# Linear attention with RMS norm, then a gated feed-forward block: token-major attention, one GELU per tile, per-batch token blocks, a written order

## The chip, the core and the metric

One core of one Trainium2 chip runs the whole kernel. The metric is the time of one execution on the device, in microseconds (us). Five engines run their own instruction streams and meet at semaphores: TensorE (PE; its weight loads are listed as PEld), VectorE (DVE), ScalarE (ACT), GpSimd (POOL) and SyncE (SP). TensorE writes its results to PSUM, from which ACT and DVE read them.

## What is computed

```python
def _attn_ref(q, k, v, g_norm):          # 8 batches, 8 heads, 576 tokens, head size 64
    kv = np.einsum('bhsd,bhse->bhde', k, v)
    out = np.einsum('bhsd,bhde->bhse', q, kv)
    rms = np.sqrt(np.mean(out * out, axis=-1, keepdims=True) + 1e-06)
    return (out / rms * g_norm)
# x = the heads of a token side by side: 4608 tokens x 512
def _moe_ref(x, w_gate, w_val, w_out, w_res):   # 512x1536, 512x1536, 1536x512, 512x512
    g = x @ w_gate
    gelu = 0.5 * g * (1.0 + erf(g / sqrt(2)))
    ffn_out = gelu * (x @ w_val) @ w_out
    res_gate = 1.0 / (1.0 + np.exp(-(x @ w_res)))
    return x + res_gate * ffn_out
```

All inputs and the output are float32 in memory; the loads convert to fp16, in which the matrix products run.

## The kernel before

**Attention** (`attention_batch`, L189 to L248) works channel-major. Per batch, POOL issues fifteen loads: q in five token chunks of 128, 128, 128, 128 and 64 rows (L195), then k (L200) and v (L204) alternating over the same chunks. q has two buffers, k and v have one each. For each of four pairs of heads, TensorE sums k^T v over the five chunks (L212), DVE masks the two cross-head blocks and multiplies by g_norm (L220), TensorE transposes q (L223) and ACT copies the transpose out (L225). For each half of the 576 tokens follow the product with q (L229, channels on the partitions), a copy (L231) and a square (L234) on DVE, a matmul that sums the squares over the channels of a head and spreads the sum back (L236), and a copy (L237). At the end of the batch ACT takes Ln and Exp of all these sums (L238, L240), with a table load for each, and DVE multiplies and so writes `xT` (L243): 512 channels by all 4608 tokens, kept for the whole run.

**Feed-forward.** Tokens go in nine blocks of 512, which do not fall on batch borders. `moe_gval` (L111 to L151) takes twelve slices of 128 of the 1536 hidden units. A slice has four matmuls for the gate (L121), four for the value (L130), a copy of the gate on ACT (L138), gate times value on DVE (L140), the square of the gate on POOL (L142), two DVE steps (L144, L148), a Sigmoid on ACT (L150) and a last product on DVE (L151): the GELU is built from a cubic and a Sigmoid. The gate and value tiles share three PSUM buffers. `moe_out` (L152 to L186) takes the four 128-token pieces of a block: twelve matmuls with w_out (L159), four with w_res (L168), four transposes that bring x back to token-major (L177), a Sigmoid (L179), a copy (L181), a product on DVE (L183), the residual add on POOL (L185) and the store on SP's queue (L186). The first two share two PSUM buffers.

**Order.** `attention_batch` 0 and 1, the four weight loads (L105 to L108, whole matrices) and `moe_gval(0)` come first; then each round has the attention of batch b+2, `moe_gval(b+1)` and `moe_out(b)`. This is the order in the program text; the framework's scheduler reorders instructions on every engine by priority and by what it takes to be ready.

Of the kernel before, what the change touches and what calls it, by code (L numbers as in the profile page):

```python
# [19 lines left out]
def kernel(  # L21
# [11 lines left out]
):  # L33
    nc = tc.nc
    P = nc.NUM_PARTITIONS
    B, H, S, D = q.shape
    T = B * S
# [23 lines left out]
    qt2p = ctx.enter_context(tc.tile_pool(name="qt2p", bufs=4))
    moep = ctx.enter_context(tc.tile_pool(name="moep", bufs=2))
    finp = ctx.enter_context(tc.tile_pool(name="finp", bufs=2))

    pmoe = ctx.enter_context(tc.tile_pool(name="pmoe", bufs=3, space=bass.MemoryType.PSUM))
    pattn = ctx.enter_context(tc.tile_pool(name="pattn", bufs=1, space=bass.MemoryType.PSUM))

    ident32 = consts.tile([P, P], FP32, tag="ident32")
    make_identity(nc, ident32)
    ident = consts.tile([P, P], FP16, tag="ident")  # L70
    nc.vector.tensor_copy(out=ident, in_=ident32)

    gcol = consts.tile([P, 1], FP32, tag="gcol")
    nc.sync.dma_start(out=gcol[0:D, :], in_=g_norm.unsqueeze(1))
    nc.sync.dma_start(out=gcol[D : 2 * D, :], in_=g_norm.unsqueeze(1))
    ginv2 = consts.tile([P, 1], FP32, tag="ginv2")
    nc.vector.tensor_tensor(out=ginv2, in0=gcol, in1=gcol, op=ALU.mult)
    nc.vector.reciprocal(out=ginv2, in_=ginv2)

    jmask = consts.tile([P, P], FP32, tag="jmask")  # L80
    nc.gpsimd.memset(jmask, 0.0)
    nc.vector.memset(jmask[0:D, 0:D], 1.0)
# [7 lines left out]
    JG = consts.tile([P, P], FP16, tag="JG")  # L90
    nc.vector.tensor_tensor(out=JG, in0=jmask, in1=grow.rearrange("p a d -> p (a d)"), op=ALU.mult)
    JIG2 = consts.tile([P, P], FP16, tag="JIG2")
    nc.vector.tensor_scalar(
        out=JIG2, in0=jmask, scalar1=ginv2[:, 0:1], scalar2=None, op0=ALU.mult
    )
    eps_col = consts.tile([P, 1], FP32, tag="eps_col")
    nc.vector.memset(eps_col, RMS_EPS)

    wg16 = wpool.tile([P, 4, F], FP16, tag="wg16")
    wv16 = wpool.tile([P, 4, F], FP16, tag="wv16")  # L100
# [12 lines left out]

    def moe_gval(J: int):
        t0 = 512 * J
        hid = hidp.tile([P, NF, 512], FP16, tag="hid")
        hids[J] = hid
        for Fi in range(NF):
            gps = pmoe.tile([P, 512], FP32, tag="gval")
            for cc in range(4):  # L120
                nc.tensor.matmul(  # L121
                    gps,
                    lhsT=wg16[:, cc, Fi * P : (Fi + 1) * P],
                    rhs=xT[:, cc, t0 : t0 + 512],
                    start=(cc == 0),
                    stop=(cc == 3),
                )
            vps = pmoe.tile([P, 512], FP32, tag="gval")
            for cc in range(4):
                nc.tensor.matmul(  # L130
                    vps,
                    lhsT=wv16[:, cc, Fi * P : (Fi + 1) * P],
                    rhs=xT[:, cc, t0 : t0 + 512],
                    start=(cc == 0),
                    stop=(cc == 3),
                )
            g16 = moep.tile([P, 512], FP16, tag="g16")
            nc.scalar.copy(out=g16, in_=gps)  # L138
            gv = moep.tile([P, 512], FP16, tag="gv")
            nc.vector.tensor_tensor(out=gv, in0=g16, in1=vps, op=ALU.mult)  # L140
            x2 = moep.tile([P, 512], FP16, tag="x2")
            nc.gpsimd.tensor_tensor(out=x2, in0=g16, in1=g16, op=ALU.mult)  # L142
            w3 = moep.tile([P, 512], FP16, tag="w3")
            nc.vector.tensor_scalar(  # L144
                out=w3, in0=x2, scalar1=B_CUBE, scalar2=1.0, op0=ALU.mult, op1=ALU.add
            )
            z3 = moep.tile([P, 512], FP16, tag="z3")
            nc.vector.tensor_tensor(out=z3, in0=w3, in1=g16, op=ALU.mult)  # L148
            sg = moep.tile([P, 512], FP16, tag="sg")
            nc.scalar.activation(out=sg, in_=z3, func=AF.Sigmoid, scale=A_SIG)  # L150
            nc.vector.tensor_tensor(out=hid[:, Fi, :], in0=gv, in1=sg, op=ALU.mult)  # L151
    def moe_out(J: int):  # L152
        t0 = 512 * J
        hid = hids[J]
        for tci in range(4):
            tt0 = t0 + 128 * tci
            fps = pmoe.tile([P, 512], FP32, tag="fr", bufs=2)
            for Fi in range(NF):
                nc.tensor.matmul(  # L159
                    fps,  # L160
                    lhsT=hid[:, Fi, tci * 128 : (tci + 1) * 128],
                    rhs=wo16[:, Fi, :],
                    start=(Fi == 0),
                    stop=(Fi == NF - 1),
                )
            rps = pmoe.tile([P, 512], FP32, tag="fr", bufs=2)
            for cc in range(4):
                nc.tensor.matmul(  # L168
                    rps,
                    lhsT=xT[:, cc, tt0 : tt0 + 128],  # L170
                    rhs=wr16[:, cc, :],
                    start=(cc == 0),
                    stop=(cc == 3),
                )
            xps = pattn.tile([P, 4, 128], FP16, tag="ort", bufs=2)
            for cc in range(4):
                nc.tensor.transpose(xps[:, cc, :], xT[:, cc, tt0 : tt0 + 128], ident)  # L177
            sig = finp.tile([P, 512], FP32, tag="sig")
            nc.scalar.activation(out=sig, in_=rps, func=AF.Sigmoid)  # L179
            xsb = finp.tile([P, 512], FP16, tag="xsb")  # L180
            nc.scalar.copy(out=xsb, in_=xps)  # L181
            pf = finp.tile([P, 512], FP32, tag="pf")
            nc.vector.tensor_tensor(out=pf, in0=fps, in1=sig, op=ALU.mult)  # L183
            osb = finp.tile([P, 512], FP32, tag="osb")
            nc.gpsimd.tensor_tensor(out=osb, in0=pf, in1=xsb, op=ALU.add)  # L185
            nc.sync.dma_start(out=out[tt0 : tt0 + 128, :], in_=osb)  # L186
# [103 lines left out]
```

## Time and profile before

| what | value |
|---|---|
| median of 3 runs | 538.26 us (538.15 to 538.30) |
| span of the profiled execution, first to last instruction | 536.4 us |
| mean granted TensorE clock, share of full | 0.954 |
| matmuls, of 512 columns / of fewer | 1440 / 592 |
| busy share PE, DVE, ACT, POOL | 76%, 66%, 48%, 49% |

The profile gives a span; the execution as timed is longer by what lies around the span. A busy PE is not PE at its peak, because matmuls overlap: what a matmul costs in a dense stretch is read from the distance between the starts of groups.

### The profile page before, as it was taken

How to read it: one execution, taken by the hardware profiler on the slowest of the kernel's cores; microseconds unless marked ns; L12 is line 12 of the kernel's file. 1: busy time of each engine (PE TensorE's matmuls, PEld its weight loads, DVE VectorE, ACT ScalarE, POOL GpSimd, SP SyncE). 2: the span in 40 equal slices, each digit the busy share in tenths (PEclk: the TensorE clock that was granted, in tenths of full speed). 3: DMA queues.
4: the chain of work that ended last, by engine and by line, in shares of the span. 5: the costliest groups of instructions: out<-in, count | busy, mean ns of one | idle time of the engine just before them, and what ended most of it. 6: DMA issues, size and time to landing. Idle time of an engine off the chain costs nothing.

```text
span 536.4 us, 6023 instructions
## 1 busy us (share of the span) xinstructions
PE 405.8 (76%) x2032; PEld 189.5 (35%) x2032; DVE 355.6 (66%) x764; ACT 256.4 (48%) x368; POOL 263.6 (49%) x275
## 2 busy tenths in 40 slices
PE   0355877884998598869886889589859977987884
PEld 0121433431443244324433444235323433433442
DVE  0162887996878766956695859584958498389311
ACT  0024466458536743494248533853485344334321
POOL 8643783493469335934484448153314443343222
PEclk9999997997999898979989998999988999999999
DMA  9999990094049205930395019101000100100111
GB/s 84 149 201 172 120 107 7 5 102 47 20 61 99 34 20 66 82 24 21 69 88 36 21 59 83 7 20 40 20 1 20 59 2 0 57 23 2 39 59 60
DMA packets 121295, 29.30 MB, mean 55 GB/s; under 512 B 113584, under 2 KB 115632, under 8 KB 121264
## 3 DMA queue, kind: packets, MB, share of 16 engines
q0 software_dynamic: 115648, 19.41, 47.4%
q1 hardware_dynamic: 5616, 9.51, 4.8%
q8 instruction: 16, 0.26, 0.2%
q14 instruction: 15, 0.12, 0.1%
HBM read 38.86 MB, written 9.44 MB: 90 GB/s over the span
## 4 chain that ended last, share of the span: by engine, by line
DVE 35%; PE 26%; issue 13%; ACT 11%; POOL 7%; DMA 7%; POOLq 0%; ACTq 0%; DVEq 0%
PE fps L159 9%; DVE z L148 8%; DVE hid L151 7%; DVE w L144 6%; PE gps L121 6%; PE vps L130 4%; DVE gv L140 4%; ACT sg L150 4%; DMA wv<-in_moe_w_val_dram 3%; DVE sq L234 3%; POOL x L142 3%; DVE rbs L237 3%; PE rps L168 3%; ACT L150 3%; DVE og L231 2%
## 5 line engine op out<-in xcount | busy, mean ns | idle before, releaser
L142 POOL TENSOR_TENSOR x<-g 128x512 f16<-128x512 f16 x108 | 116.5, 1083 | 163.7 <-ACT g L138 155.9
L130 PE MATMUL vps<-xT,wv 128*128 128x512 f16 x432 | 126.6, 407 | 32.0 <-ACT g L138 31.7
L121 PE MATMUL gps<-xT,wg 128*128 128x512 f16 x432 | 124.3, 405 | 19.4 <-DVE gv L140 19.0
L150 ACT ACTIVATE sg<-z 128x512 f16<-128x512 f16 x108 | 68.0, 630 | 121.8 <-DVE z L148 121.6
L159 PE MATMUL fps<-wo,hid 128*128 128x512 f16 x432 | 103.8, 379 | 9.6 <-ACT sig L179 6.5
L185 POOL TENSOR_TENSOR osb<-pf,xsb 128x512 f32<-128x512 f32 x36 | 42.0, 1167 | 86.7 <-DVE pf L183 60.9
L138 ACT CAST g<-gps 128x512 f16<-128x512 f32 x108 | 61.5, 578 | 31.5 <-PE gps L121 28.1
L140 DVE TENSOR_TENSOR gv<-g,vps 128x512 f16<-128x512 f16 x108 | 73.2, 678 | 4.6 <-PE vps L130 3.6
L130 PEld LDWEIGHTS <-wv 128*128 128x128 f16 x432 | 42.9, 102 | 83.6 <-issue 45.7
L121 PEld LDWEIGHTS <-wg 128*128 128x128 f16 x432 | 42.7, 103 | 83.9 <-issue 48.4
L151 DVE TENSOR_TENSOR hid<-gv,sg 128x512 f16<-128x512 f16 x108 | 61.3, 568 | 16.5 <-ACT sg L150 14.6
L148 DVE TENSOR_TENSOR z<-w,g 128x512 f16<-128x512 f16 x108 | 61.7, 571 | 2.5
L159 PEld LDWEIGHTS <-hid 128*128 128x128 f16 x432 | 41.7, 98 | 59.5 <-issue 10.1
L144 DVE TENSOR_SCALAR w<-x 128x512 f16<-128x512 f16 x108 | 50.2, 466 | 8.9 <-POOL x L142 8.9
L183 DVE TENSOR_TENSOR pf<-fps,sig 128x512 f32<-128x512 f32 x36 | 24.7, 687 | 41.7 <-ACT sig L179 41.6
L212 PE MATMUL kvps<-v_sb,k_sb 128*128 128x128 f16 (+1 forms) x160 | 21.5, 231 | 30.8 <-DMA v_sb<-in_v_dram 29.3
L237 DVE COPY rbs<-rb 128x288 f32<-128x288 f32 x64 | 28.9, 451 | 20.1 <-PE rb L236 19.8
L179 ACT ACTIVATE sig<-rps 128x512 f32<-128x512 f32 x36 | 21.5, 597 | 42.3 <-PE rps L168 42.2
L200 POOL DMA_DIRECT2D k_sb<-in_k_dram x40 | 35.0, 875 | 12.8 <-PE kvps L212 10.8
L225 ACT COPY qt<-qtps 128x576 f16<-128x576 f16 x32 | 20.3, 634 | 43.7 <-PE qtps L223 43.6
L231 DVE CAST og<-otg 128x288 f16<-128x288 f32 x64 | 28.6, 447 | 18.4 <-PE otg L229 18.4
L236 PE MATMUL rb<-sq,JIG 128*128 128x288 f16 x64 | 19.7, 308 | 26.8 <-DVE sq L234 26.8
(41 smaller groups left out, 384.2 us busy)
## 6 DMA issues: line engine op xcount, KB each, us to landing
out_dram<-osb SPq DMA_DIRECT2D x36, 256.0 KB, 2.0
q_sb<-in_q_dram POOLq DMA_DIRECT2D x32, 128.0 KB, 4.4
k_sb<-in_k_dram POOLq DMA_DIRECT2D x32, 128.0 KB, 4.3
v_sb<-in_v_dram POOLq DMA_DIRECT2D x32, 128.0 KB, 4.4
wg<-in_moe_w_gate_dram POOLq DMA_DIRECT2D x1, 1536.0 KB, 12.1
wv<-in_moe_w_val_dram POOLq DMA_DIRECT2D x1, 1536.0 KB, 18.6
wo<-in_moe_w_out_dram POOLq DMA_DIRECT2D x1, 1536.0 KB, 12.8
q_sb<-in_q_dram POOLq DMA_DIRECT2D x8, 64.0 KB, 4.2
```

What stands on the lines that cost most here:

```text
L121: nc.tensor.matmul(gps, lhsT=wg16[:, cc, Fi * P : (Fi + 1) * P], rhs=xT[:, cc, t0 : t0 + 512], start=(cc == 0), stop=(cc == 3),)
L130: nc.tensor.matmul(vps, lhsT=wv16[:, cc, Fi * P : (Fi + 1) * P], rhs=xT[:, cc, t0 : t0 + 512], start=(cc == 0), stop=(cc == 3),)
L138: nc.scalar.copy(out=g16, in_=gps)
L140: nc.vector.tensor_tensor(out=gv, in0=g16, in1=vps, op=ALU.mult)
L142: nc.gpsimd.tensor_tensor(out=x2, in0=g16, in1=g16, op=ALU.mult)
L144: nc.vector.tensor_scalar(out=w3, in0=x2, scalar1=B_CUBE, scalar2=1.0, op0=ALU.mult, op1=ALU.add)
L148: nc.vector.tensor_tensor(out=z3, in0=w3, in1=g16, op=ALU.mult)
L150: nc.scalar.activation(out=sg, in_=z3, func=AF.Sigmoid, scale=A_SIG)
L151: nc.vector.tensor_tensor(out=hid[:, Fi, :], in0=gv, in1=sg, op=ALU.mult)
L159: nc.tensor.matmul(fps, lhsT=hid[:, Fi, tci * 128 : (tci + 1) * 128], rhs=wo16[:, Fi, :], start=(Fi == 0), stop=(Fi == NF - 1),)
L185: nc.gpsimd.tensor_tensor(out=osb, in0=pf, in1=xsb, op=ALU.add)
L237: nc.vector.tensor_copy(out=rbs[:, j, hh, :], in_=rb)
```

## The change

The kernel is rewritten, with the same loads from memory to fp16 and the same feed-forward products.

- Tokens are regrouped: block b (0 to 7) holds the first 512 tokens of batch b, and block 8 the last 64 tokens of each of the eight batches. k and v rests are padded with zeros to 128 rows; the rests of two batches' q share one 128-row tile.
- Attention is token-major: q is transposed, and the product (`a_o`) has tokens on the partitions. ACT copies it out and squares it, DVE reduces the square per head, and a 13-instruction DVE chain on 32 or 40 columns (`a_norm`) finds the inverse root by an integer shift and three Newton steps. Two DVE products give x (`a_x`), four transposes and an ACT copy give `xT` (`a_xT`). The matmul that summed squares, Ln and Exp are gone.
- The GELU is one ACT instruction out of PSUM and one DVE product. The gate's Sigmoid is a Tanh; two DVE instructions finish the output, and no transpose back is needed. POOL computes nothing except a set-up step: it issues loads.
- PSUM: six buffers for all feed-forward products in rotation, two for attention.
- The order is as written, on every engine (`manual_schedule`): sixteen slots per block, with a step of the next batch's attention behind the products of each slot. The loads of batch 0 come first, then the weights (gate and value in six column pieces each), then batch 1; batch b+2 is loaded from the start of block b.

Cut to its core (what was removed is shown above):

```diff
+    ctx.enter_context(tc.manual_schedule())
+    nc.scalar.preload_act_table_set("gelu_and_others")
...
+    load_batch(0)
...
+    load_weights()
+    load_batch(1)
...
+    def a_qT(b, jj):
+        ps = pattn.tile([P, 2, NP, P], FP16, tag="at", name="qtp")
+        for e in range(2):
+            j = 2 * jj + e
+            for pr in range(NP):
+                nc.tensor.transpose(ps[:, e, pr, :], q_sb[:, j, pr * P : (pr + 1) * P], ident)
+        nc.scalar.copy(out=st[b]["qT"][:, 2 * jj : 2 * jj + 2, :, :], in_=ps)
...
+    def a_kv(b):
+        ps = pattn.tile([P, NP, P], FP32, tag="at", name="kvp")
+        for pr in range(NP):
+            cs = slice(pr * P, (pr + 1) * P)
+            for j in range(NJ):
+                nc.tensor.matmul(ps[:, pr, :], lhsT=k_sb[:, j, cs], rhs=v_sb[:, j, cs], start=(j == 0), stop=False)
+            nc.tensor.matmul(ps[:, pr, :], lhsT=kr_z[b % 2][:, cs], rhs=vr_z[b % 2][:, cs], start=False, stop=True)
+        nc.vector.tensor_tensor(out=st[b]["kv2"], in0=ps, in1=mask[:, None, :].to_broadcast([P, NP, P]), op=ALU.mult)
...
+    def a_post_o(b, j, ps):
+        nc.scalar.copy(out=o32, in_=ps)
+        nc.scalar.activation(out=sq, in_=ps, func=AF.Square)
+        nc.vector.tensor_reduce(out=s["ss"][:, j, :], in_=sq, op=ALU.add, axis=mybir.AxisListType.X)
...
+    def a_norm(b):
+        nc.vector.tensor_scalar(out=m, in0=ss, scalar1=1.0 / D, scalar2=RMS_EPS, op0=ALU.mult, op1=ALU.add)
...
+        for _ in range(3):
+            nc.vector.tensor_tensor(out=a, in0=yy, in1=yy, op=ALU.mult)
+            nc.vector.tensor_tensor(out=a, in0=a, in1=mh, op=ALU.mult)
+            nc.vector.scalar_tensor_tensor(out=yy, in0=a, scalar=1.5, in1=yy, op0=ALU.add, op1=ALU.mult)
...
+            0: [lambda: attn_begin(b), lambda: a_qT(b, 0)],
+            1: [lambda: a_qT(b, 1)],
+            2: [lambda: a_kv(b)],
+            3: [lambda: a_rem_qT(b)] if odd else [],
+            4: [lambda: a_o(b, 0)],
+            5: [lambda: a_o(b, 1)],
+            6: [lambda: a_o(b, 2)],
+            7: [lambda: a_o(b, 3)],
+            8: [lambda: a_rem_o(b)] if odd else [],
+            9: [lambda: a_norm(b), lambda: a_x(b, 0)],
+            10: [lambda: a_x(b, 1)],
+            11: [lambda: a_x(b, 2), lambda: a_xT(b, 0)],
+            12: [lambda: a_x(b, 3), lambda: a_xT(b, 1)],
+            13: [lambda: a_xT(b, 2)] + ([lambda: a_x(b, 4)] if odd else []),
+            14: [lambda: a_xT(b, 3)],
+            15: [lambda: a_xT(b, 4)] if odd else [],
...
+    def m_gval(blk, f):
...
+        nc.scalar.activation(out=ge, in_=gps, func=AF.Gelu)
+        nc.vector.tensor_tensor(out=hids[blk][:, f, :], in0=ge, in1=vps, op=ALU.mult)
...
+        nc.scalar.activation(out=th, in_=rps, func=AF.Tanh, scale=0.5)
+        nc.vector.scalar_tensor_tensor(out=pf, in0=th, scalar=1.0, in1=fps, op0=ALU.add, op1=ALU.mult)
+        nc.vector.scalar_tensor_tensor(out=osb, in0=pf, scalar=0.5, in1=x_t[blk][:, j, :], op0=ALU.mult, op1=ALU.add)
...
+    for blk in range(B + 1):
+        nxt = blk + 1
...
+        if blk + 2 < B:
+            load_batch(blk + 2)
+        for s in range(16):
+            if s < NF:
+                m_gval(blk, s)
+            else:
+                m_out(blk, s - NF)
+            for f in plan.get(s, []):
+                f()
```

In `m_out` the four products with w_res come ahead of the twelve with w_out. The steps of batch 0's attention run by themselves, ahead of block 0.

## Rows read from the trace of the kernel before

**Rows 1.** The page's busy time, share of the span and instructions of each engine.
```profile
PE 405.8 (76%) x2032; PEld 189.5 (35%) x2032; DVE 355.6 (66%) x764; ACT 256.4 (48%) x368; POOL 263.6 (49%) x275
```
**Rows 2.** Waits of the whole run: who waited for whom, total us, times, longest.
```profile
POOL x L142 <- ACT g L138: 155.9, 72, 11.6
ACT sg L150 <- DVE z L148: 121.6, 80, 3.9
...
PE rb L236 <- DVE sq L234: 26.8, 29, 2.3
```
**Rows 3.** Groups by line and form: busy us, mean ns | idle before, releasers.
```profile
L121 PE MATMUL gps<-xT,wg 128*128 128x512 f16 x432 | 124.3, 405 | 19.4 <-DVE gv L140 19.0
L142 POOL TENSOR_TENSOR x<-g 128x512 f16<-128x512 f16 x108 | 116.5, 1083 | 163.7 <-ACT g L138 155.9 <-DVE rbs L237 3.6 <-DVE hid L151 3.1
...
L140 DVE TENSOR_TENSOR gv<-g,vps 128x512 f16<-128x512 f16 x108 | 73.2, 678 | 4.6 <-PE vps L130 3.6
...
L179 ACT ACTIVATE sig<-rps 128x512 f32<-128x512 f32 x36 | 21.5, 597 | 42.3 <-PE rps L168 42.2
...
L225 ACT COPY qt<-qtps 128x576 f16<-128x576 f16 x32 | 20.3, 634 | 43.7 <-PE qtps L223 43.6
```
**Rows 4.** Timeline of PE in a dense stretch: start us, us, instructions merged.
```profile
303.19 2.75 PE L159 MATMUL fps<-wo,hid 128*128 128x512 f16 x12
305.78 1.03 PE L168 MATMUL rps<-wr,xT 128*128 128x512 f16 x4
306.65 0.61 PE L177 MATMUL xps<-ident,xT 128*128 128x128 f16 x8
307.09 0.33 PE L212 MATMUL kvps<-v_sb,k_sb 128*128 128x128 f16 x3
```
**Rows 5.** Timeline of POOL: the last weight load issued.
```profile
44.39 0.77 POOL L108 DMA_DIRECT2D wr<-in_moe_w_res_dram  x1
```
**Rows 6.** DMA issues by line: count, KB each, median us from issue to landing.
```profile
wr<-in_moe_w_res_dram POOLq DMA_DIRECT2D x1, 512.0 KB, 14.8
```
**Rows 7.** Busy time of the engines in stretches, granted clock, DMA share and rate.
```profile
10.00:17.00 7.00, 0.53 (x2) 0.20 (x2) 0.00 (x0) 0.00 (x0) 6.55 (x9) 1.00 2.36 150
...
50.00:54.00 4.00, 4.00 (x15) 1.62 (x14) 0.93 (x2) 1.23 (x2) 1.04 (x1) 1.00 1.24 207
...
406.00:535.00 129.00, 106.03 (x513) 47.64 (x511) 76.25 (x130) 47.54 (x85) 46.85 (x44) 1.00 0.09 33
```
**Rows 8.** Waits of PE in that last stretch, 406 to 535 us.
```profile
PE gps L121 <- DVE gv L140: 11.9, 17, 1.0
PE fps L159 <- ACT sig L179: 6.3, 8, 1.9
```
**Rows 9.** Timeline of PE after its long wait for the first loads.
```profile
47.78 0.63 PE L121 MATMUL gps<-xT,wg 128*128 128x512 f16 x1
...
52.23 1.80 PE L121 MATMUL gps<-xT,wg 128*128 128x512 f16 x4
```
**Rows 10.** Timeline at the start: DVE's set-up steps, and a sum of batch 0.
```profile
3.94 0.16 DVE L78 RECIPROCAL ginv<-ginv 128x1 f32<-128x1 f32 x1
4.14 0.29 DVE L93 TENSOR_SCALAR JIG<-jmask,ginv 128x128 f16<-128x128 f32 x1
...
22.07 0.26 PE L212 MATMUL kvps<-v_sb,k_sb 64*128 64x128 f16 x1 [1.29 <-DMA v_sb<-in_v_dram]
```
**Rows 11.** Timeline of the end.
```profile
531.03 0.69 DVE L183 TENSOR_TENSOR pf<-fps,sig 128x512 f32<-128x512 f32 x1 [3.61 <-ACT sig L179]
531.80 1.15 POOL L185 TENSOR_TENSOR osb<-pf,xsb 128x512 f32<-128x512 f32 x1 [3.14 <-DVE pf L183]
```
**Rows 12.** Timeline of the value and GELU steps, DVE at its undisturbed rate.
```profile
499.20 0.43 DVE L148 TENSOR_TENSOR z<-w,g 128x512 f16<-128x512 f16 x1
```
**Rows 13.** Span and mean granted TensorE clock.
```profile
core 0: 536.4 us, clock 0.954
```

More of the change, by code (lines that the diff above doesn't have):

```diff
@@ L36 @@
     B, H, S, D = q.shape
-    T = B * S
     C = H * D
@@ L61 @@
[L61 to L68, printed above, removed]
+    moep = ctx.enter_context(tc.tile_pool(name="moep", bufs=3))
@@ new lines @@
+    finp = ctx.enter_context(tc.tile_pool(name="finp", bufs=3))
+    pmoe = ctx.enter_context(tc.tile_pool(name="pmoe", bufs=6, space=bass.MemoryType.PSUM))
+    pattn = ctx.enter_context(tc.tile_pool(name="pattn", bufs=2, space=bass.MemoryType.PSUM))
+    ctx.enter_context(tc.manual_schedule())
+    nc.scalar.preload_act_table_set("gelu_and_others")
+    kr_z, vr_z = [], []
+    for i in range(2):
+        kz = consts.tile([P, C], FP16, name=f"kr{i}")
+        vz = consts.tile([P, C], FP16, name=f"vr{i}")
+        nc.vector.memset(kz[R:P, :], 0.0)
+        nc.vector.memset(vz[R:P, :], 0.0)
+        kr_z.append(kz)
+        vr_z.append(vz)
@@ L69 @@
+    wg_c, wv_c = [], []
+    for i in range(F // WC):
+        wg_c.append(wpool.tile([P, NP, WC], FP16, name=f"wg{i}"))
+        wv_c.append(wpool.tile([P, NP, WC], FP16, name=f"wv{i}"))
+    wo16 = wpool.tile([P, NF, C], FP16, name="wo16")
+    wr16 = wpool.tile([P, NP, C], FP16, name="wr16")
+    load_batch(0)
+    ident32 = consts.tile([P, P], FP32, name="ident32")
     make_identity(nc, ident32)
-    ident = consts.tile([P, P], FP16, tag="ident")
+    ident = consts.tile([P, P], FP16, name="ident")
@@ L71 @@
     nc.vector.tensor_copy(out=ident, in_=ident32)
[L73 to L82, printed above, removed]
@@ L89 @@
     )
[L90 to L100, printed above, removed]
@@ L112 @@
-    hids = {}
[L114 to L145, printed above, removed]
-            )
[L147 to L186, printed above, removed]
@@ L250 @@
-    attention_batch(0)
-    attention_batch(1)
-    load_weights()
-    moe_gval(0)
-    for b in range(B + 1):
-        if b + 2 < B:
-            attention_batch(b + 2)
-        if b + 1 <= B:
-            moe_gval(b + 1)
-        moe_out(b)
+    g16 = consts.tile([P, C], FP16, name="g16")
+    nc.vector.tensor_copy(out=g16, in_=grow.rearrange("p h d -> p (h d)"))
+    qtr = []
+    for i in range(2):
+        t = consts.tile([P, NP, P], FP16, name=f"qtr{i}")
+        nc.vector.memset(t, 0.0)
+        qtr.append(t)
@@ new lines, in load_weights @@
+    def load_weights():
+        for i in range(F // WC):
+            cs = slice(i * WC, (i + 1) * WC)
+            nc.gpsimd.dma_start(out=wg_c[i], in_=moe_w_gate[:, cs].rearrange("(cc p) f -> p cc f", p=P))
+            nc.gpsimd.dma_start(out=wv_c[i], in_=moe_w_val[:, cs].rearrange("(cc p) f -> p cc f", p=P))
+        nc.gpsimd.dma_start(out=wr16, in_=moe_w_res.rearrange("(cc p) c -> p cc c", p=P))
+        nc.gpsimd.dma_start(out=wo16, in_=moe_w_out.rearrange("(ff p) c -> p ff c", p=P))
+    load_weights()
@@ new lines, in a_post_o, with a_o @@
+    def a_post_o(b, j, ps):
+        s = st[b]
+        o32 = attnp.tile([P, C], FP32, tag="o32", bufs=6, name="o32")
+        nc.scalar.copy(out=o32, in_=ps)
+        sq = attnp.tile([P, H, D], FP32, tag="sq", name="sq")
+        nc.scalar.activation(out=sq, in_=ps, func=AF.Square)
+        nc.vector.tensor_reduce(out=s["ss"][:, j, :], in_=sq, op=ALU.add, axis=mybir.AxisListType.X)
+        s["o"][j] = o32
+    def a_o(b, j):
+        s = st[b]
+        ps = pattn.tile([P, C], FP32, tag="at", name="op")
+        for pr in range(NP):
+            nc.tensor.matmul(
+                ps[:, pr * P : (pr + 1) * P], lhsT=s["qT"][:, j, pr, :], rhs=s["kv2"][:, pr, :], start=True, stop=True
+            )
+        a_post_o(b, j, ps)
@@ new lines, in a_rem_qT, with a_rem_o @@
+    def a_rem_qT(b):
+        qr = qr_t[b // 2]
+        ps = pattn.tile([P, NP, P], FP16, tag="at", name="qtrp")
+        for pr in range(NP):
+            nc.tensor.transpose(ps[:, pr, :], qr[:, pr * P : (pr + 1) * P], ident)
+        nc.scalar.copy(out=qtr[0][:, :, 0:R], in_=ps[:, :, 0:R])
+        nc.scalar.copy(out=qtr[1][:, :, R : 2 * R], in_=ps[:, :, R : 2 * R])
+    def a_rem_o(b):
+        ps = pattn.tile([P, C], FP32, tag="at", name="orp")
+        for pr in range(NP):
+            for e in range(2):
+                nc.tensor.matmul(
+                    ps[:, pr * P : (pr + 1) * P],
+                    lhsT=qtr[e][:, pr, :],
+                    rhs=st[b - 1 + e]["kv2"][:, pr, :],
+                    start=(e == 0),
+                    stop=(e == 1),
+                )
+        a_post_o(b, NJ, ps)
@@ new lines, in where, with a_x @@
+    def where(b, j):
+        return (b, j) if j < NJ else (B, b // 2)
+    def a_x(b, j):
+        s = st[b]
+        blk, jj = where(b, j)
+        t16 = attnp.tile([P, H, D], FP16, tag="t16", name="t16")
+        nc.vector.tensor_tensor(
+            out=t16,
+            in0=s["o"][j].rearrange("p (h d) -> p h d", h=H),
+            in1=s["rinv"][:, j, :, None].to_broadcast([P, H, D]),
+            op=ALU.mult,
+        )
+        nc.vector.tensor_tensor(
+            out=x_t[blk][:, jj, :], in0=t16.rearrange("p h d -> p (h d)"), in1=g16, op=ALU.mult
+        )
@@ new lines, in a_xT, with attn_slots @@
+    def a_xT(b, j):
+        blk, jj = where(b, j)
+        ps = pattn.tile([P, NP, P], FP16, tag="at", name="xtp")
+        for cc in range(NP):
+            nc.tensor.transpose(ps[:, cc, :], x_t[blk][:, jj, cc * P : (cc + 1) * P], ident)
+        nc.scalar.copy(out=xT_t[blk][:, :, jj * P : (jj + 1) * P], in_=ps)
+    def attn_slots(b):
+        odd = b % 2 == 1
+        plan = {
+            0: [lambda: attn_begin(b), lambda: a_qT(b, 0)],
[14 more added lines that the diff above has]
+            15: [lambda: a_xT(b, 4)] if odd else [],
+        }
+        return plan
@@ new lines, in m_out @@
+    def m_out(blk, j):
+        hid = hids[blk]
+        js = slice(j * P, (j + 1) * P)
+        rps = pmoe.tile([P, C], FP32, tag="mm", name="rps")
+        for cc in range(NP):
+            nc.tensor.matmul(
+                rps, lhsT=xT_t[blk][:, cc, js], rhs=wr16[:, cc, :], start=(cc == 0), stop=(cc == NP - 1)
+            )
+        fps = pmoe.tile([P, C], FP32, tag="mm", name="fps")
+        for f in range(NF):
+            nc.tensor.matmul(fps, lhsT=hid[:, f, js], rhs=wo16[:, f, :], start=(f == 0), stop=(f == NF - 1))
+        th = finp.tile([P, C], FP32, tag="th", name="th")
+        nc.scalar.activation(out=th, in_=rps, func=AF.Tanh, scale=0.5)
+        pf = finp.tile([P, C], FP32, tag="pf", name="pf")
+        nc.vector.scalar_tensor_tensor(out=pf, in0=th, scalar=1.0, in1=fps, op0=ALU.add, op1=ALU.mult)
+        osb = finp.tile([P, C], FP32, tag="osb", name="osb")
+        nc.vector.scalar_tensor_tensor(
+            out=osb, in0=pf, scalar=0.5, in1=x_t[blk][:, j, :], op0=ALU.mult, op1=ALU.add
+        )
+        if blk < B:
+            r0 = blk * S + j * P
+            nc.sync.dma_start(out=out[r0 : r0 + P, :], in_=osb)
+        else:
+            for e in range(2):
+                r0 = (2 * j + e) * S + M0
+                nc.sync.dma_start(out=out[r0 : r0 + R, :], in_=osb[e * R : (e + 1) * R, :])
@@ new lines @@
+    new_block(B)
+    new_block(0)
+    plan = attn_slots(0)
+    for s in range(16):
+        for f in plan[s]:
+            f()
+    for blk in range(B + 1):
+        nxt = blk + 1
+        plan = {}
+        if nxt < B:
+            new_block(nxt)
+            plan = attn_slots(nxt)
+        if blk + 2 < B:
+            load_batch(blk + 2)
+        for s in range(16):
+            if s < NF:
+                m_gval(blk, s)
+            else:
+                m_out(blk, s - NF)
+            for f in plan.get(s, []):
+                f()
```

169 lines of the change are left out of this document (85 added, 84 removed).

## The prediction

> **What bounds the kernel now.** I began with the busy shares [rows 1]: no engine is full, PE leads with 76%. Next what PE would need: in a dense stretch twelve 512-column matmuls start over 2.59 us and four over 0.87, so 0.216 us each, and eight transposes take 0.44, so 0.055 each [rows 4]. The 1440 wide matmuls cost 1440 x 0.216 = 311 us. So some 200 us of the span are start-up, narrow matmuls and waits of PE. The waits [rows 2] show whose: POOL waits for the gate's copy 72 times, ACT waits for DVE's `z` 80 times, up to 3.9 us. That is one loop, ACT, DVE, POOL, DVE, ACT, DVE, walked 108 times for the GELU, and POOL's square alone takes 1083 ns [rows 3]. The gate and value tiles have three buffers, so PE waits for the loop (L121's idle time, 19.4 us before DVE's `gv`, is one face of it [rows 3]). In attention PE waits for DVE's square before each head sum, 26.8 us in 29 waits [rows 2]. The kernel is bound by hand-offs, over a floor that PE sets.
>
> **The change, part by part.**
>
> *GELU and output.* Per slice go a copy, POOL's square and four DVE steps; in come one ACT instruction out of PSUM and one DVE product. No Gelu is in the trace: I take the Sigmoid out of PSUM, 597 ns, same shape and engine [rows 3], for Tanh and Square too; it would have to take three times as long to reach PE's pace per slice, and could at best save nothing. The product reads PSUM as `gv` does, 678 ns [rows 3]. A slice gives PE 8 x 0.216 = 1.73 us, so both fit under it, and six PSUM buffers let PE run three slices ahead. If two tables were needed (Gelu, Tanh), ACT would reload twice a block, 18 times in all; ACT has the room, below. The transposes back and POOL's add go; DVE's two output steps and the per-head reduction, forms that the trace lacks, are taken as `pf`, 0.69 each [rows 11] (from 0.43 [rows 12] to POOL's 1.15 for the add [rows 11]; at either end DVE stays under PE), and lie under a piece's 16 x 0.216 = 3.46 us.
>
> *Attention.* Per batch PE gets 16 transposes of q, 20 matmuls for the sum, 16 for the product, 16 transposes of x, and per pair of batches 4 + 8 + 4 for the rests: 8 x 68 + 4 x 16 = 608 narrow ones. At 0.055 they cost 33.4 us. PE's whole work is 344 us.
>
> *Cover on the other engines.* ACT: 16 x 0.6 per block; per batch two copies of 1024 columns, about 1.0 each (634 ns at 576 columns [rows 3]), and 12 to 17 passes at 0.6: about 9 x 9.6 + 8 x 10.6 = 171 us. DVE: per block 12 x 0.68 + 8 x 0.69 = 13.7, per batch about 11: 211 us. POOL only issues loads. Each stays under PE's 344, also slot by slot (ACT's worst slots, 4 to 7, hold three passes, 1.8 us, against PE's 1.73 + 4 x 0.055 = 1.95), but for slot 9.
>
> *Slot 9.* There DVE runs product, the 13 small steps, then `a_x(0)` (0.69 + 0.42 [rows 11, 12]); PE wants its result after slots 10 and 11, 3.46 us later. A small DVE step starts 0.20 us after the one before it (3.94 to 4.14) and takes up to 0.29 at 128 columns [rows 10]; 40 columns lie near the first, so 13 x 0.2 = 2.6. From the end of slot 9's matmuls DVE needs 0.15 + 0.68 + 2.6 + 1.11 + 0.05 = 4.6, and PE waits 1.1 us, in 7 batches: 7.7 us. By the bounds (0.19 and 0.31 a step) 1.0 to 2.5 each, 7 to 17.5. Queued behind the chain on DVE are the products of slots 10 and 11; they end 2.3 us after `a_x(0)`, before PE's twelfth w_out product asks for the last one 3.2 us after it. The other steps of attention have one to four slots (1.7 us and more) between hand-offs of about 0.9 us each (26.8 / 29 [rows 2]).
>
> *Start.* In-order PE stands in block 0's slot 2 until batch 1's k and v are in, and these are now queued behind the weights on POOL's queue. Before, batches 0 and 1 and the weights were all in at 44.39 + 14.8 = 59.2 us [rows 5, 6]; the same bytes go in another order, and only q's rest follows what PE waits for. I take 59. The gate and value pieces now have shorter rows (512 bytes in fp16): 1 KB rows ran at 207 GB/s, the 128-byte rows of q, k, v at 150 [rows 7]. 3.1 MB at 150 instead of 207 cost 5.8 us more; I take none, as the 150 GB/s stand beside a POOL busy 6.55 of 7 us with issuing, so it need not be the row length. Batch 0's attention, alone and in order, needs after its loads (about 21 us; the last in the old order was used at 22.07 [rows 10]) about 2 + 0.8 + 0.5 + 4.8 + 0.7 + 2.6 + 4.4 + 1.2 = 17 us, to 38; it ends before the wait and costs nothing. After a long wait PE runs as at the lower of its two clocks, 1.2 of 2.4 GHz: at 47.78 a matmul takes 0.63 instead of 0.38, and four starting at 52.23 still 1.80 instead of 1.03 [rows 4, 9]. About 6 us at half rate lose 3.
>
> *Clock later on.* From 406 us on the clock was full although PE waited 25 times, 0.7 us on average and up to 1.9 [rows 7, 8], so I charge the 1.1 us waits nothing more. The Trainium skill (TensorE: Matmul & The Clock Gate, "A second HAM failure mode: psum-queue depth-cycling") describes the opposite for 512-column matmuls whose outputs cycle through PSUM banks, as this rotation of six does: small gaps that let the clock fall again and again. By that rule the sum would be 427 (rivals).
>
> *End.* After the last w_out product: two DVE steps, 0.2 + 2 x 0.69, then the store and closing as before: the last add ends at 531.80 + 1.15 = 532.95, the span at 536.4 [rows 1, 11, 13], 3.5. In all 5.1; the last piece has two stores, 0 to 1 more.
>
> **Sum.** PE's work ahead of the wait: three slices, 24 x 0.216 = 5.2, and 84 narrow ones, 4.6; left 344.4 - 9.8 = 334.6. 59 + 334.6 + 7.7 + 3 + 5.1 = 409.4 us of span, against 536.4. The runs' median, 538.3, lies 1.9 above that span: 411, 24% less.
>
> **Rivals.**
>
> *Clock falls in the rotation.* Mean granted clock now 0.954 [rows 13]. If PE, busy with little else but matmuls, keeps that, its 345 us lose 4.6%: 16 us, 427. For it: the gaps at slot 9, and the skill's rule. Against: the last 129 us before, with 18% of PE's time idle and the clock full [rows 7].
>
> *PE waits at every hand-off.* The written order gives PE nothing else to run when a step's input is late. With some 12 groups of attention in each of 7 batches and 0.9 us each [rows 2], 84 x 0.9 = 76 us: 487. For it: PE no longer skips ahead. Against: a slot of 1.73 us covers 0.9.
>
> *The woven attention is not covered at all (slower).* Place: slots 0 to 15 of blocks 0 to 6. Before, batch 0's chain took from 22.07 to the first gate product at 47.78, 25.7 us [rows 9, 10]. If each of 7 batches held PE up that long, less its own 4.2 us of PE work: 7 x 21.5 = 150, so 561. It decides the sign from (538 - 411) / 7 = 18 us per batch. Against: the chain's ACT and DVE work is 21 us a batch and has 16 slots, 34.6 us, of PE work beside it.
>
> *The change does not do what it says:* the order is not kept, or both tables alternate. 18 reloads fall into ACT's idle half; 411 to 416, inside the range.
>
> **How the numbers follow.** Forecast 0.64, with its own range of 401 (no wait at slot 9) to 433 (slow pieces 6, slot 9 another 10, second store 1, some of the unforeseen 5). Clock 0.12, inside that. Table or order 0.04, inside. Hand-offs 0.14, of which the milder half, up to 450, is in the range. Slower 0.06. So 400 to 448 leaves out about 0.13. What a measurement of this kernel can tell from no change is about 0.2%, 1 us: faster 0.93, same 0.01, slower 0.06.
>
> **What would show it.** PE stands in its first wait until about 59 us and is then dense: blocks with attention of 39 to 40 us, the last two of 34.6, starts of wide matmuls 0.216 apart, one wait of about 1 us per block for `x` from DVE, ahead of the transposes of slot 11. ACT near 171 us busy, DVE near 211, POOL with load issues only, one table load. Wrong would be: a wait for loads past 65 us; granted clock below 0.97 after 70; PE waiting in slots 0 to 8; DVE above 300 us.

## The result, and the profile after

The changed kernel takes 421.4 us (median of 5; 420.0 to 423.8) against 538.3: ratio 0.7835, 95% interval 0.7813 to 0.7856. Forecast were 411 us and a range of 400 to 448. The median lies 10.4 us above the forecast. The profiled execution, the slowest of the five, has a span of 422.0 us, 12.6 above the forecast sum of 409.4.

First the page's parts 1 and 2 of the changed kernel, which answer to [rows 1]: busy time and share of each engine, then the span in 40 slices of 10.6 us.

```profile
PE 358.7 (85%) x2048; PEld 179.5 (43%) x2048; DVE 213.0 (50%) x411; ACT 161.1 (38%) x277; POOL 112.2 (27%) x140
...
PE   0052457979998999899899989998999899999994
```

PE is now the full engine from the seventh slice to the end (70% and more, the last slice apart), and at most half busy before. DVE at 213.0 us and ACT at 161.1 are where the cover needed them (211 and 171 were reckoned).

The waits of PE in the changed kernel, the longest of the whole run (who waited for whom; total us, times, longest), answer to [rows 2, 8].

```profile
PEld L165 <- DMA q_sb<-in_q_dram: 26.7, 3, 17.7
PE qtp L165 <- DVE ident L112: 24.6, 1, 24.6
...
PE xtp L264 <- DVE x L256: 17.4, 11, 6.0
```

All but one kind belong to the start. The second is PE's first wait: POOL builds the identity matrix for the transposes only behind its fifteen load issues of batch 0, at 23.67 us, although q is in at 17.7. Of the 17.4 us for x, 7.4 are batch 0's chain ahead of block 0; from 70 us on, PE waits for nothing else than x, seven times, once per later batch:

```profile
PE xtp L264 <- DVE x L256: 10.0, 7, 3.0
```

(That is PE's whole list of waits from 70 us to the end.) The next lines, of the timeline of PE in the changed kernel, stand against [rows 4]: one block boundary and one wait.

```profile
105.76 1.03 PE L299 MATMUL gps<-xT,wg 128*128 128x512 f16 x4
106.63 1.03 PE L304 MATMUL vps<-xT,wv 128*128 128x512 f16 x4
107.49 0.61 PE L165 MATMUL qtp<-ident,q_sb 128*128 128x128 f16 x8
...
130.69 0.40 PE L264 MATMUL xtp<-ident,x 128*128 128x128 f16 x4 [1.14 <-DVE x L256]
...
145.41 1.03 PE L299 MATMUL gps<-xT,wg 128*128 128x512 f16 x4
```

Wide matmuls start 0.216 us apart, narrow ones 0.055, across every change from one to the other. The block takes 145.41 - 105.76 = 39.65 us; the next, with the transposes and products of the rests, ends at 186.02 and takes 40.6.

Last the start, the timeline of POOL in the changed kernel, against [rows 5, 10].

```profile
4.87 3.54 POOL L88 DMA_DIRECT2D k_sb<-in_k_dram  x4
17.92 3.50 POOL L90 DMA_DIRECT2D v_sb<-in_v_dram  x4 [9.52 <-DMA q_sb<-in_q_dram]
...
36.71 1.02 POOL L137 DMA_DIRECT2D wo<-in_moe_w_out_dram  x1 [0.57 <-DMA wv<-in_moe_w_val_dram]
...
54.88 0.88 POOL L88 DMA_DIRECT2D k_sb<-in_k_dram  x1 [6.19 <-DMA wo<-in_moe_w_out_dram]
55.74 3.52 POOL L90 DMA_DIRECT2D v_sb<-in_v_dram  x4
```

POOL stands 9.5 us after its eighth load, until the first load of q has landed at 17.9. In the kernel before, the wait at the same place was 1.2 us:

```profile
9.70 0.88 POOL L204 DMA_DIRECT2D v_sb<-in_v_dram  x1 [1.20 <-DMA q_sb<-in_q_dram]
```

Later in the changed kernel the last loads of batch 1 stand behind w_out. PE resumes here (timeline of PE, changed kernel):

```profile
66.72 0.26 PE L175 MATMUL kvp<-vr,kr 128*128 128x128 f16 x1 [0.68 <-DMA vr<-in_v_dram]
```

### The profile page after: what moved, and what is told of

Its sections match the earlier page's. It is cut to its first block, busy times and chain, and to the rows that moved or that the text cites. A ratio compares the mean times of both kernels' runs of the same rounds, so it can differ in the third digit from the quotient of the medians.

```text
span 422.0 us, 5322 instructions
## 1 busy us (share of the span) xinstructions
PE 358.7 (85%) x2048; PEld 179.5 (43%) x2048; DVE 213.0 (50%) x411; ACT 161.1 (38%) x277; POOL 112.2 (27%) x140
## 4 chain that ended last, share of the span: by engine, by line
PE 73%; DMA 12%; DVE 8%; POOL 3%; issue 1%; ACT 1%; DVEq 0%; POOLq 0%
PE fps L321 22%; PE gps L299 18%; PE vps L304 18%; PE rps L316 7%; DMA wo<-in_moe_w_out_dram 4%; DMA q_sb<-in_q_dram 4%; PE xtp L264 2%; DMA wv<-in_moe_w_val_dram 2%; POOL v_sb L90 2%; DMA vr<-in_v_dram 2%; PE kvp L174 2%; PE op L193 1%; PE qtp L165 1%; DVE t L250 1%; DVE hid L309 1%
## 5 line engine op out<-in xcount | busy, mean ns | idle before, releaser
L309 DVE TENSOR_TENSOR hid<-ge,vps 128x512 f16<-128x512 f16 x108 | 74.2, 687 | 82.0 <-PE vps L304 81.7
L308 ACT ACTIVATE ge<-gps 128x512 f16<-128x512 f32 x108 | 64.8, 600 | 84.0 <-PE gps L299 80.6
L86 POOL DMA_DIRECT2D q_sb<-in_q_dram x32 | 28.4, 913 | 108.6 <-PE qtp L165 104.0
L326 DVE SCALAR_TENSOR_TENSOR pf<-th,fps 128x512 f32<-128x512 f32 x36 | 24.8, 689 | 60.2 <-PE fps L321 60.2
L316 PE MATMUL rps<-wr,xT 128*128 128x512 f16 x144 | 37.3, 382 | 0.0
L186 DVE TENSOR_REDUCE ss<-sq 128x8 f32<-128x512 f32 x36 | 24.7, 686 | 21.9 <-ACT sq L185 21.9
L324 ACT ACTIVATE th<-rps 128x512 f32<-128x512 f32 x36 | 21.5, 598 | 27.5 <-PE rps L316 27.5
L90 POOL DMA_DIRECT2D v_sb<-in_v_dram x32 | 28.6, 956 | 9.5 <-DMA q_sb<-in_q_dram 9.5
L264 PE MATMUL xtp<-ident,x 128*128 128x128 f16 x144 | 14.9, 229 | 17.4 <-DVE x L256 17.4
L328 DVE SCALAR_TENSOR_TENSOR osb<-pf,x 128x512 f32<-128x512 f32 x36 | 24.9, 692 | 1.2
L250 DVE TENSOR_TENSOR t<-o,ny 128x512 f16<-128x512 f32 x36 | 24.7, 686 | 0.3
## 6 DMA issues: line engine op xcount, KB each, us to landing
wo<-in_moe_w_out_dram POOLq DMA_DIRECT2D x1, 1536.0 KB, 17.9
```

The costliest lines, as they stand in the source:

```text
L86: nc.gpsimd.dma_start(out=q_sb[:, j, :].rearrange("p (h d) -> p h d", h=H), in_=src)
L90: nc.gpsimd.dma_start(out=v_sb[:, j, :].rearrange("p (h d) -> p h d", h=H), in_=src)
L250: nc.vector.tensor_tensor(out=t16, in0=s["o"][j].rearrange("p (h d) -> p h d", h=H), in1=s["rinv"][:, j, :, None].to_broadcast([P, H, D]), ...
L308: nc.scalar.activation(out=ge, in_=gps, func=AF.Gelu)
L309: nc.vector.tensor_tensor(out=hids[blk][:, f, :], in0=ge, in1=vps, op=ALU.mult)
L316: nc.tensor.matmul(rps, lhsT=xT_t[blk][:, cc, js], rhs=wr16[:, cc, :], start=(cc == 0), stop=(cc == NP - 1))
```

## The experiments

The first four ran on one chip; the scheduler's order, the two with a GELU exchanged and the first of the three edits together on a second; the three buffers and the last two on a third. Each ran beside the kernel before (538.6, 537.9 and 539.7 us).

**The base again**, no edit.

> The changed kernel again, as the base for the three edits beside it: 421 us (420 to 424), matmuls of batch 1's k-v sum ending near 67 us, seven waits of PE for x from DVE of about 1.4 us each.

Measured: 421.2 us (0.7825, 0.7797 to 0.7852), PE's wait for x 10.0 us in seven times. The edits below are compared with this. The last wait of its start:

```profile
65.70 0.22 PE L175 MATMUL kvp<-vr,kr 128*128 128x128 f16 x1 [0.68 <-DMA vr<-in_v_dram]
```

**A shorter load of g_norm.**

```diff
-    grow = consts.tile([P, H, D], FP32, name="grow")
-        in_=bass.AP(tensor=g_norm.tensor, offset=g_norm.offset, ap=[[0, P], [0, H], [1, D]]),
-    nc.vector.tensor_copy(out=g16, in_=grow.rearrange("p h d -> p (h d)"))
+    grow = consts.tile([P, D], FP32, name="grow")
+        in_=bass.AP(tensor=g_norm.tensor, offset=g_norm.offset, ap=[[0, P], [1, D]]),
+    for h in range(H):
+        nc.vector.tensor_copy(out=g16[:, h * D : (h + 1) * D], in_=grow)
```

> One edit: g_norm is loaded as 64 columns and spread over the eight heads by DVE, so SP's load has 128 short packets instead of 1024. Theory A (that load's packets hold back the first loads of batch 0): first packets of q before 5 us instead of 13.7, POOL's 9.5 us wait ahead of v gone, batch 1's k-v sum some 8 us earlier (58 to 59 us), time 413 (411 to 415). Rival (POOL's first loads are slow to start whatever SP does): first packets still at 12 to 14 us, time unchanged at 421.

Measured: 412.8 us (0.7668, 0.7650 to 0.7686), 8.4 less. The DMA issues first of the changed kernel, then of this one (KB, us to landing):

```profile
grow<-in_g_norm_dram SPq DMA_DIRECT2D x1, 256.0 KB, 16.1
```

```profile
grow<-in_g_norm_dram SPq DMA_DIRECT2D x1, 32.0 KB, 2.9
```

then POOL's timeline in this one, where v follows k without a wait, and PE's last wait of the start:

```profile
4.86 3.54 POOL L88 DMA_DIRECT2D k_sb<-in_k_dram  x4
8.32 3.58 POOL L90 DMA_DIRECT2D v_sb<-in_v_dram  x4
...
56.03 0.27 PE L176 MATMUL kvp<-vr,kr 128*128 128x128 f16 x1 [0.57 <-DMA vr<-in_v_dram]
```

The DMA engines move 96 GB/s from 3 to 5 us here; in the changed kernel 13 up to 5 us, and 94 only from 14 to 16. Theory A holds: SP's copy of one 256-byte row to 128 partitions, eight times over, held the first loads up. Its price on the whole run is 8.4 us. Why 1024 such packets take 16 us was not tried.

**Batch 1 ahead of w_res and w_out**, whose loads are taken out of load_weights into a function of their own.

```diff
     load_weights()
     load_batch(1)
+    load_late_weights()
```

> One edit: batch 1's loads go ahead of w_res and w_out. Theory A (PE's start is held by the bytes queued ahead of batch 1; 2.1 MB at 207 GB/s are 10 us): the k-v sum of batch 1 ends near 57 us, time 411 (409 to 414), and w_out, asked for near 75 us, is in by 67. Rival (the start is bound by all bytes together): PE waits as long for w_out in slot 12, time within 2 us of 421.

Measured: 408.0 us (0.7576, 0.7564 to 0.7588), 13.2 less, more than the 10 of the bytes and just beyond Theory A's range. Its PE timeline shows the last wait of the start and no wait for w_out behind it:

```profile
55.42 0.22 PE L178 MATMUL kvp<-vr,kr 128*128 128x128 f16 x1 [0.58 <-DMA vr<-in_v_dram]
```

That is 10.3 us earlier than 65.70 in the base. The rest: PE's seven waits for x sum to 8.6 us instead of 10.0, the longest 1.5 instead of 2.9, and the granted clock, 0.58 from 66 to 70 us and 0.68 from 90 to 95 in the base, is 1.00 from 55 us to the end. These two stretches cost the base some 3.3 us. Theory A's cause holds: the bytes queued ahead of batch 1.

**The first transposes of x one slot later.**

```diff
-            11: [lambda: a_x(b, 2), lambda: a_xT(b, 0)],
-            12: [lambda: a_x(b, 3), lambda: a_xT(b, 1)],
+            11: [lambda: a_x(b, 2)],
+            12: [lambda: a_x(b, 3), lambda: a_xT(b, 0), lambda: a_xT(b, 1)],
```

> One edit: the first transposes of x move from slot 11 to slot 12, behind a piece's output products. Theory A (PE waits there only because DVE's 13-step chain ends 1.4 us after PE arrives): the seven waits go and nothing else gets late, 7 x 1.4 = 10 us, time 411 (410 to 413). Rival (DVE is late for all that follows it, so the wait moves to the output products that need the last slices): the idle time shows up ahead of the w_out products, time within 2 us of 421.

Measured: 414.7 us (0.7692, 0.7667 to 0.7718), 6.6 less, between the two theories, outside both ranges and nearer to A. The whole list of PE's waits from 75 us on in this kernel:

```profile
PE fps L321 <- DVE hid L309: 3.0, 8, 1.3
```

The seven waits for x are gone, and 3.0 of their 10.0 us came back where the rival said, ahead of the w_out products: DVE does the second x between the products of slots 10 and 11.

**The scheduler's order for the changed kernel.**

```diff
-    ctx.enter_context(tc.manual_schedule())
+    pass
```

> One edit: the written order is dropped and the framework's scheduler orders the changed kernel's instructions, as it did before. Theory A (the order is worth something: PE needs other work between an attention step and the next that depends on it): PE's waits for ACT and DVE grow from about 18 us to 40 us and more, time 435 to 470. Rival (the shorter loops alone give the gain, any order covers them): time within 6 us of 421.

Measured: 409.4 us (0.7608, 0.7595 to 0.7620): both expectations missed; the written order costs 12 us against the scheduler's. PE's whole list of waits from 68 us on:

```profile
PE xtp L264 <- DVE x L256: 2.4, 7, 0.6
```

In this order the waits for x shrink from 10.0 to 2.4 us, and PE does not stand in front of batch 1's sum. Its timeline:

```profile
62.62 0.22 PE L174 MATMUL kvp<-v_sb,k_sb 128*128 128x128 f16 x1 [1.27 <-DMA v_sb<-in_v_dram]
62.68 0.81 PE L299 MATMUL gps<-xT,wg 128*128 128x512 f16 x3
63.41 0.22 PE L174 MATMUL kvp<-v_sb,k_sb 128*128 128x128 f16 x1
63.47 1.02 PE L304 MATMUL vps<-xT,wv 128*128 128x512 f16 x4
```

Gate and value products, 17 from 62.68 on or 3.7 us of work, fill the gaps between the chunks of k and v, where the written order has PE wait.

**The GELU alone, in the kernel before.**

```diff
-            nc.scalar.copy(out=g16, in_=gps)
...
-            nc.vector.tensor_tensor(out=hid[:, Fi, :], in0=gv, in1=sg, op=ALU.mult)
+            nc.scalar.activation(out=g16, in_=gps, func=AF.Gelu)
+            nc.vector.tensor_tensor(out=hid[:, Fi, :], in0=g16, in1=vps, op=ALU.mult)
```

> The kernel before with one part of the change alone: the GELU as one table instruction out of PSUM and one DVE product, attention, order and buffers as before. Its Gelu and the gate's Sigmoid need different tables, so ACT has up to some 100 table loads of 1.28 us. Theory A (the GELU's loop over three engines was most of PE's loss): 440 to 470 us, POOL no longer in any chain. Rival (attention's hand-offs and the start hold the time, the loop is only where the waits are booked): over 500 us.

Measured: 440.3 us (0.8176, 0.8153 to 0.8198), 98 of the 117 us. Groups by line of this kernel: the table loads that the mixture of Gelu and Sigmoid costs, and PE's value products (busy us, mean ns | idle before); last a wait of PE, which answers to [rows 2].

```profile
L130 PE MATMUL vps<-xT,wv 128*128 128x512 f16 x432 | 119.5, 384 | 11.7 <-ACT g L138 11.6
...
L138 ACT ACT_TABLE_LOAD x39 | 50.0, 1283 | 1.0 <-PE gps L121 0.3
...
L167 ACT ACT_TABLE_LOAD x25 | 32.1, 1283 | 0.5
...
PE rb L224 <- DVE sq L222: 3.9, 4, 1.0
```

81 table loads, 104 us of ACT, in all lines; they mostly stay beside PE's work (PE waits 11.6 us for ACT's `g` and 3.6 for its `sig`). Theory A holds: the GELU over three engines was most of the loss. But the edit takes away more than the loop's length. DVE's busy time falls from 355.6 to 187.6 us, the mean of the attention's square from 555 to 315 ns, and with it PE's wait for that square from 26.8 to 3.9 us. How much was the loop and how much the load that it put on DVE was not separated. Nor was the attention rewritten by itself: of the other 19 us only the buffers and the order have runs of their own, below and above.

**The old GELU in the changed kernel** (copy, gate times value, square, two DVE steps, Sigmoid, product; the gate's Tanh kept). The table set loaded at the start is the Sigmoid's; ACT still loads one table in the whole run.

```diff
-        nc.scalar.activation(out=ge, in_=gps, func=AF.Gelu)
-        nc.vector.tensor_tensor(out=hids[blk][:, f, :], in0=ge, in1=vps, op=ALU.mult)
+        nc.scalar.copy(out=g16_, in_=gps)
...
+        nc.scalar.activation(out=sg, in_=z3, func=AF.Sigmoid, scale=1.5957691216057308)
+        nc.vector.tensor_tensor(out=hids[blk][:, f, :], in0=gv, in1=sg, op=ALU.mult)
```

> The changed kernel with the old GELU put back (copy, POOL's square, DVE's three steps, Sigmoid, product; the gate's Tanh unchanged). Theory A (in a written order ACT's copy of the next slice stands behind the Sigmoid of this one, so a slice costs the whole loop: 0.58 + 1.08 + 0.28 + 0.42 + 0.63 and hand-offs, 3.2 us against PE's 1.73): 12 x 3.2 + 13.8 = 52 us a block, 530 to 560 in all, no better than before. Rival (six PSUM buffers cover the loop, DVE is the bound at about 40 to 45 us a block): 440 to 480.

Measured: 615.2 us (1.1439, 1.1419 to 1.1459), slower than the kernel before, and slower than Theory A's 560. ACT's timeline shows the loop:

```profile
204.56 0.59 ACT L308 CAST ge<-gps 128x512 f16<-128x512 f32 x1
207.08 0.63 ACT L318 ACTIVATE sg<-z 128x512 f16<-128x512 f16 x1 [1.94 <-DVE z L316]
207.62 0.57 ACT L308 CAST ge<-gps 128x512 f16<-128x512 f32 x1
```

This slice takes 207.62 - 204.56 = 3.06 us, as reckoned; the one before it, with a copy of the attention between, took 3.96. PE's timeline shows the last output products of three blocks, the first two blocks with attention beside them, the third without:

```profile
439.33 2.75 PE L331 MATMUL fps<-wo,hid 128*128 128x512 f16 x12
...
501.58 2.75 PE L331 MATMUL fps<-wo,hid 128*128 128x512 f16 x12
...
553.09 2.75 PE L331 MATMUL fps<-wo,hid 128*128 128x512 f16 x12
```

A block without attention takes 51.5 us, near the 52 reckoned for all; one with attention takes 61 to 62, of which the reckoning had nothing. Seven times 10 us is most of what Theory A lacks: attention's steps now hang in the same queues (PE waits 71.1 us for x). The mean granted clock is 0.89; its share was not separated. Whether the scheduler's order would cover the long loop here was not run.

**Three PSUM buffers instead of six.**

```diff
-    pmoe = ctx.enter_context(tc.tile_pool(name="pmoe", bufs=6, space=bass.MemoryType.PSUM))
+    pmoe = ctx.enter_context(tc.tile_pool(name="pmoe", bufs=3, space=bass.MemoryType.PSUM))
```

> One edit to the changed kernel: three PSUM buffers for the feed-forward products instead of six. Theory A (with the short loop a value tile is free 0.9 us after its last matmul, and PE asks for its buffer 1.73 us after; only behind slot 9, where DVE is late, does PE wait some 0.6 us more per batch): 425 us (421 to 430). Rival (the six buffers are a main part of the gain): 440 or more, with PE waiting for ACT or DVE in most slices.

Measured: 422.2 us (0.7818, 0.7786 to 0.7851), no different from 421.2. The extra wait behind slot 9 did not show: PE's only waits after 70 us are again for x.

```profile
PE xtp L264 <- DVE x L256: 10.2, 7, 3.1
```

The buffers beyond three buy nothing here.

**Start and slot 9 mended together**, with the shorter load of g_norm from above.

```diff
-    load_weights()
+    load_pieces(range(0, 3))
     load_batch(1)
+    load_pieces(range(3, F // WC))
+    load_late_weights()
...
-            10: [lambda: a_x(b, 1)],
-            11: [lambda: a_x(b, 2), lambda: a_xT(b, 0)],
-            12: [lambda: a_x(b, 3), lambda: a_xT(b, 1)],
+            10: [],
+            11: [lambda: a_x(b, 1), lambda: a_x(b, 2)],
+            12: [lambda: a_x(b, 3), lambda: a_xT(b, 0), lambda: a_xT(b, 1)],
```

> Three edits together: g_norm as 64 columns; loads in the order batch 0, three column pieces of gate and value, batch 1, the other pieces, w_res and w_out; the second x step moved to slot 11 and the first transposes of x to slot 12. Theory A (start and slot 9 are what was left above PE's work): batch 0's attention ends near 33 us, PE is dense from there, 33 + 3 cold + 331 of work + 5, about 384 us (381 to 390). Rival (PE then meets the next wait, for column pieces or w_out still on the way): 395 or more, with idle time of PE before 75 us named after a weight load.

Measured: 384.6 us (0.7150, 0.7134 to 0.7166), 9% below the changed kernel. Its stretches (us; busy time and count of PE, PEld, DVE, ACT and POOL; granted clock, DMA share, GB/s):

```profile
33.00:50.00 17.00, 16.39 (x107) 8.68 (x107) 6.07 (x9) 9.17 (x16) 13.06 (x17) 0.89 1.64 189
50.00:378.00 328.00, 326.36 (x1877) 162.66 (x1873) 192.20 (x366) 142.21 (x247) 69.56 (x84) 1.00 0.62 65
```

PE is busy 326.36 of 328 us, and its one wait after 60 us, for x, is 0.2. What it still waits lies ahead of 33 us; the first wait there, 14.9 us, is again for the identity matrix, while q is in at 4.8. It ran once more, as the base for the same kernel under the scheduler:

> The three edits together again, in the written order, as the base for the run beside it: 384.6 us (383 to 386).

> The three edits with the framework's scheduler instead of the written order. Theory A (what the scheduler's order gained before, 12 us, was the wait at slot 9 and the start, both mended here by hand): 385 us, within 4. Rival (it gains on something else too): 378 or less.

Measured: 384.8 us in the written order (0.7131, 0.7110 to 0.7151) and 384.9 under the scheduler (0.7141, 0.7115 to 0.7166). Once the two places are mended, the order makes no difference.

## Why the prediction was right, and what was mis-sized

**Right: what bounded, and what bounds.** The GELU's loop of hand-offs was read from the waits; its removal, with the load that it put on DVE, gives 98 us alone, and its return in the written order takes more than everything back. PE's price list held: from its release at 66.72 PE runs to the last twelve w_out products,

```profile
413.02 2.75 PE L321 MATMUL fps<-wo,hid 128*128 128x512 f16 x12
```

which end at 415.6 with 12 x 0.216; less 10.0 us of waits and 3.0 of half clock, that is 335.9 us of work against 334.6. Blocks take 39.65 or 40.6 us with attention (39 to 40 forecast) and 34.5 without (34.6). Two slips in the working changed nothing: 536 less 311 is 225 us, not some 200, and the forecast without slot 9's 7.7 is 403, not 401.

**Mis-sized: the term of 59 us for the start.** It was 66.7, 7.7 of the 12.6 us missing. The step read: the same bytes go in another order, so they are in when they were in before. The same bytes they were not: SP's g_norm load had grown from 64 KB to 256 KB, an exception to the "same loads" of the change, and it goes ahead of POOL's first load (0.74 us against 1.25). Cut to 32 KB by itself, it gives back 8.4 us, and the start's last wait ends at 56.03 instead of 65.70. So the growth is more than the whole 7.7: without it the start would have been 3 us shorter than the 59 taken, for reasons that were not separated. One of the prediction's four signs of being wrong did come, a wait for loads past 65 us (66.72, and 65.70 in the base); the other three did not. The other doubt in that term, shorter rows of the weight pieces, was rightly held small: the windows of the changed kernel have 191 GB/s while the pieces run and 207 in the rows of w_out, so 3.1 MB took about 1 us more, not the 5.8 that 150 GB/s would cost.

```profile
28.00:42.00 14.00, 5.20 (x41) 3.81 (x40) 9.00 (x25) 5.06 (x10) 10.00 (x13) 1.00 1.43 191
45.00:52.00 7.00, 2.89 (x7) 0.73 (x5) 0.69 (x1) 0.60 (x1) 1.48 (x2) 1.00 1.24 207
```

**Mis-sized a little: slot 9**, 10.0 us instead of 7.7, inside its bounds. Where nothing disturbs DVE, the wait is 1.14 us, or 1.22 with 40 columns, near the 1.1 reckoned. The longest, 3.0, is batch 1's, below. **The end** took 6.4 us from the last product instead of 5.1 (two stores had been given 0 to 1). **The clock** cost 3.0, as taken, but by luck: the half clock (1.2 GHz) after the wait for loads cost 1.3 from the release on, and the other 1.7 came after the 3.0 us wait at slot 9, for which nothing had been charged. Ahead of 66 us matmuls ran at half pace too (four in 1.91 us at 45.98, where the profile's granted clock still reads 1.00); there PE waits for loads anyway.

```profile
66.00:69.40 3.40, 2.72 (x20) 2.21 (x20) 0.69 (x1) 0.00 (x0) 3.40 (x5) 0.50 1.98 126
...
89.90:93.30 3.40, 3.40 (x10) 1.18 (x9) 2.42 (x5) 0.85 (x2) 0.00 (x0) 0.50 0.52 33
93.30:421.00 327.70, 315.40 (x1807) 156.20 (x1804) 181.02 (x337) 135.74 (x234) 50.31 (x60) 1.00 0.43 51
```

Start 7.7, slot 9 2.3, clock 0, end 1.3 and PE's work 1.3 make the 12.6.

**The rivals.** The clock did not fall in the rotation: it is full for 327.7 us with six buffers in turn and six waits of 1.1 to 1.2 us among them, and with three buffers from 95 to 418 us. The Trainium skill (TensorE: Matmul & The Clock Gate, "A second HAM failure mode: psum-queue depth-cycling") describes a TensorE that idles briefly and often between groups while its outputs cycle through PSUM banks. No run here shows that: groups follow each other at 0.216 us per matmul, so the rotation made no such gaps, and the rule as the prediction applied it is not borne out.

PE did not wait at every hand-off either: slots 0 to 8 show no wait after the start. But that rival's reason, that a written order leaves PE nothing else to run when an input is late, was right at two places, the start and slot 9, and costs 12 us against the scheduler's order. The slower rival did not come true: a block with attention takes 5 to 6 us more than one without, and 4.2 of that is PE's own work. With the old GELU the difference is 10 us.

## What to carry to other kernels

Price the engine that will bound by the distance between starts in a dense stretch, and then look for the few places where it must still stand: the first loads and the longest chain on another engine. In a written order, put a step that depends on such a chain behind work that needs nothing from it, and queue loads in the order in which they are asked for. A small load on another queue is to be counted too: here 256 KB of one repeated row, against 32 KB, cost 8.4 us.

## What was not expected of the hardware

Four of DVE's small steps took three to five times as long in one batch (the fourth, L236, 0.77 us). DVE's and POOL's timelines of the changed kernel, batch 1:

```profile
82.96 3.69 POOL L90 DMA_DIRECT2D v_sb<-in_v_dram  x4
83.43 0.61 DVE L229 TENSOR_SCALAR nm<-ss 128x40 f32<-128x40 f32 x1
84.08 0.84 DVE L230 TENSOR_SCALAR na<-nm 128x40 int32<-128x40 int32 x1
84.95 0.84 DVE L233 TENSOR_SCALAR ny<-na 128x40 int32<-128x40 int32 x1
...
85.83 0.20 DVE L238 TENSOR_TENSOR na<-ny 128x40 f32<-128x40 f32 x1
```

and batch 2, no load being issued:

```profile
127.02 0.18 DVE L230 TENSOR_SCALAR na<-nm 128x32 int32<-128x32 int32 x1
```

The one-input steps last about as long as POOL's issue of one load beside them (3.69 us for four), and the two-input ones, in the same stretch, do not (0.20). This lengthens batch 1's wait at slot 9 from 1.2 to 3.0 us.

The other traces bear it out. In the ten of the changed kernel and its variants without the old GELU, the 251 one-input steps of this chain during which POOL did nothing took 0.17 to 0.19 us each. All 35 that took longer than 0.25 (up to 0.84) overlap an issue of POOL; 34 more overlap one and take at most 0.21. With the old GELU, step L230 takes 1.04 us in seven batches, each time beside POOL's square, also 1.04. The loads' place in time was not moved by itself. The Trainium skill (SBUF — State Buffer, "Who interferes with whom") says that one-input operations like this can take a pair of ports that VectorE shares with GpSimd, whoever comes second being blocked for the whole instruction, and that GpSimd needs it to write the descriptors of its loads (the last partly inferred there); the rows agree.
